# The last 64 queries of two experts in one tile of 128 rows (fused attention and mixture of experts)

## The chip, the cores and the metric

The kernel runs on one core of one Trainium2 chip. The metric is the device time of one execution in microseconds; the median of several executions counts.

## The reference

Three blocks follow each other on 4 batches of 576 tokens: a sparse attention of 8 heads, a mixing block with sines and cosines, and a mixture of four attention experts, of which each token uses two. Only the last block matters for the change:

```python
logits = x @ w_gate                       # (4, 576, 4)
topk = np.argpartition(-logits, 2, axis=-1)[..., :2]
...
for e in range(4):
    q, k, v = x @ wq[e], x @ wk[e], x @ wv[e]        # 64 wide
    scores = scale * (q @ k.transpose(0, 2, 1))
    scores = np.where(causal, -1000000000.0, scores)
    scores = scores - scores.max(-1, keepdims=True)
    a = np.exp(scores)
    a /= a.sum(-1, keepdims=True) + 1e-09
    ye = a @ v @ wo[e]
    ...
        out += mask[..., None] * w[:, :, kk:kk + 1] * ye
```

Every expert attends causally over 576 tokens, and its rows are scaled by the gate before they are added up.

## The kernel before, in words

The matrix products are done in a 32-bit format of reduced precision, and each operand is split into a high part and a low remainder, so that most products are three matmuls (hi hi, lo hi, hi lo; the helper `mm3`, lines 241 to 243). In the experts, q carries its high part in 64 partitions and its low part in the other 64; k is written twice beside that, and `klow` holds k's remainder beside 64 partitions of zeros, which are cleared once at the start of the expert stage (line 413, on POOL).

The first 382 us are the other two blocks. Then comes the expert stage, batch by batch, in `experts`. Per batch and pair of experts (m = 0, 1), `project_qk` makes q and k of both experts; then `attention` runs once per expert e. It goes over five tiles of queries, four of 128 rows and the last, t = 4, of 64. Per tile PE makes the scores (lines 514 and 515, for t = 4 in two chunks of 288 keys) and adds the causal mask by a matmul with the identity as weights (line 517). DVE takes the row maximum (519), ACT the exponential with its sum (530), DVE finishes the sum and its reciprocal (534, 535), and POOL (for t = 0 DVE) multiplies by that and by the gate (537). PE transposes the tile block by block (540) into PSUM, ACT copies it out as `pthi` (548), and DVE makes the remainder `ptlo` (549). After the five tiles PE multiplies with the values (560, 564) in two halves of 288 queries; line 569 and 570 add the two parts of v. For t = 4, all of this has 64 rows:

```python
w, t0 = TW[t], 128 * t              # TW = [128, 128, 128, 128, 64]
...
nc.tensor.matmul(s[:w, t0 - c0:t0 - c0 + w], identb[:, :w], mask_c[:, :w], ...)
...
nc.tensor.transpose(tp[:, c * w:(c + 1) * w], p[:w, 128 * c:128 * c + 128], ident[:w, :w])
```

Between the tiles stand `fill` units: the projections of the next pair and batch (`pv`, `pq`) and the output projections of the batch before (`po`), spread over 20 slots per batch. Eight output projections remain for the end. Each is copied by ACT (596) into one of four staging slots in `X[0]`, from which SP issues the store.

Names on PE: `th`, `y`, `g` belong to the mixing block, `pv`, `pq`, `po` to projections, `s` to scores, `tp` to transposes, `o` to values. The order of the instructions on each engine is set by a scheduler that plans the whole program at once when it is built. So a change in the last stage, or two copies at the start, can move rows in stages that the diff does not touch.

Of the kernel before, what the change touches and what calls it, by code (L numbers as in the profile page):

```python
# [42 lines left out]
def fused_kernel(ctx: ExitStack, tc: tile.TileContext, ql, kl, vl, qs, ks, vs, wth, wtk, wch, wqk, wvg, wo, out):  # L43
# [42 lines left out]
    select(mask_c, [[-1, 128]], 0, 1)  # L86

# [321 lines left out]
    xproj, vs, qks, moved = {}, {}, {}, []  # L409
    klow = [[cw.tile([128, S], F32R, name=f"klow_{j}_{i}") for i in range(2)] for j in range(3)]  # L410
    for j in range(3):
        for i in range(2):
            nc.gpsimd.memset(f(klow[j][i][64 - 64 * i:128 - 64 * i, :]), 0.0)

    def project_v(b):
# [7 lines left out]
        vs[b] = vc, cp.tile([128, NT, 4], F32, tag="gt", name=f"gt_{b}")  # L423
# [17 lines left out]
    def gates(b, lg):  # L441
# [20 lines left out]
        nc.vector.tensor_tensor(gt, gt, mx[:, :, 1:2].to_broadcast([128, NT, 4]), op=ALU.mult)  # L462

    def project_qk(b, m):
        q = [cp.tile([128, S], F32R, tag="q", bufs=6, name=f"q_{b}_{m}_{i}") for i in range(2)]
# [5 lines left out]
        def unit(part, n):  # L473
# [21 lines left out]
    def attention(b, e, of, fill):  # L495
        vc, gt = vs[b]
        q, k, kl = qks[b, e]
        pr = slice(64 * (e % 2), 64 * (e % 2) + 64)

        pthi = cp.tile([128, 2368], F32R, tag="pthi", name=f"pthi_{b}_{e}")  # L500
        ptlo = cp.tile([128, 2368], F32R, tag="ptlo", name=f"ptlo_{b}_{e}")
        sm = cp.tile([128, NT], F32, tag="sm", name=f"sm_{b}_{e}")
        nm = cp.tile([128, 8], F32, tag="nm", name=f"nm_{b}_{e}")
        for t in range(NT):
            w, t0 = TW[t], 128 * t
            ts = slice(t0, t0 + w)
            kn = t0 + w
            p = cp.tile([128, 640], F32, tag="p", bufs=4, name=f"p_{b}_{e}_{t}")
            chunks = [(0, kn)] if t < 4 else [(0, HALF), (HALF, S)]
            scs = []  # L510
            for ci, (c0, c1) in enumerate(chunks):
                s = ps2.tile([128, 512], F32, tag="s", bufs=3, name=f"s_{b}_{e}_{t}_{ci}")
                last = ci == len(chunks) - 1
                nc.tensor.matmul(s[:w, :c1 - c0], q[:, ts], k[:, c0:c1], start=True, stop=False)
                nc.tensor.matmul(s[:w, :c1 - c0], q[:, ts], kl[:, c0:c1], start=False, stop=not last)
                if last:
                    scored = nc.tensor.matmul(s[:w, t0 - c0:t0 - c0 + w], identb[:, :w], mask_c[:, :w],  # L517
                                              start=False, stop=True)
                nc.vector.tensor_reduce(nm[:w, t + ci:t + ci + 1], s[:w, :c1 - c0], axis=AX.X, op=ALU.max,  # L519
                                        negate=True)  # L520
                scs.append(s)
            with tc.issue_after(scored.ins):
                for unit in fill[t]:
                    unit()
            if t == 4:
                nc.vector.tensor_tensor(nm[:w, 4:5], nm[:w, 4:5], nm[:w, 5:6], op=ALU.min)
                nc.gpsimd.memset(p[:w, S:640], 0.0)
            for ci, (c0, c1) in enumerate(chunks):
                acc = sm[:w, t:t + 1] if ci == 0 else nm[:w, 6:7]
                nc.scalar.activation(p[:w, c0:c1], scs[ci][:w, :c1 - c0], AF.Exp, bias=nm[:w, t:t + 1], scale=1.0,  # L530
                                     accum_out=acc)
            if t == 4:
                nc.vector.tensor_tensor(sm[:w, 4:5], sm[:w, 4:5], nm[:w, 6:7], op=ALU.add)
            nc.vector.tensor_scalar_add(sm[:w, t:t + 1], sm[:w, t:t + 1], 1e-9)
            nc.vector.reciprocal(sm[:w, t:t + 1], sm[:w, t:t + 1])  # L535
            eng = nc.vector if t == 0 else nc.gpsimd
            eng.tensor_scalar(p[:w, :kn], p[:w, :kn], sm[:w, t:t + 1], gt[:w, t, e:e + 1], op0=ALU.mult, op1=ALU.mult)  # L537
            tp = ps2.tile([128, 512], F32, tag="t", bufs=2, name=f"tp_{b}_{e}_{t}")
            for c in range(t + 1):
                nc.tensor.transpose(tp[:, c * w:(c + 1) * w], p[:w, 128 * c:128 * c + 128], ident[:w, :w])  # L540
            src = tp[:, :(t + 1) * w].rearrange("p (n q) -> p n q", q=w)

            def dst(v):
                if t == 0:
                    return v[:, None, :w]
                return v[:, 128:128 + 448 * (t + 1)].rearrange("p (n q) -> p n q", q=448)[:, :, t0 - 128:t0 - 128 + w]
# [151 lines left out]
```

## Time and profile before

| | |
|---|---|
| median of three runs | 601.68 us (598.15 to 605.10) |
| the profiled execution | 603.8 us, its span 602.0 us |
| mean granted TensorE clock | 0.968 of full |
| busy over the span: PE, weight loads, DVE, ACT, POOL | 95%, 87%, 70%, 57%, 41% |
| expert stage | about 382 to 602 us |

The span runs from the first to the last instruction of the profiled execution; every row of the trace counts from its start. A row of the timeline tells when an instruction began, how long it is counted as busy, its engine, line and operation, and what it writes and reads. "PE" are matmuls, "PEld" their weight loads. Ends of matmuls are modelled and overlap the next, so how fast PE works is read from one start to the next. A bracket at the end tells how long the engine had been idle and which instruction ended that.

### The profile page before, as it was taken

Reading aid. Unit: us, or ns where it says so; the run is one execution under the profiler, and the core shown is the slowest. Engines: PE = TensorE matmul, PEld = TensorE weight load, DVE = VectorE, ACT = ScalarE, POOL = GpSimd, SP = SyncE. Lnnn points to the kernel's source line nnn. Section 1 sums busy time; section 2 is a strip of 40 time slices with the busy share of each in tenths; the row PEclk is TensorE's granted clock in tenths of the full one; section 3 lists DMA queues with packets and bytes.
Section 4 is the critical chain, followed back from the end, with each engine's and each line's share of the span. In section 5 each row is a group of like instructions: output and inputs, shape, how many; then the busy total and the mean of one; then the engine's idle time right before and its main releaser. Section 6 shows DMA issues by size and latency. Waiting matters only on the chain.

```text
span 602.0 us, 12582 instructions
## 1 busy us (share of the span) xinstructions
PE 571.9 (95%) x4560; PEld 525.3 (87%) x4560; DVE 422.5 (70%) x1209; ACT 340.7 (57%) x935; POOL 244.5 (41%) x336
## 2 busy tenths in 40 slices
PE   7985979899999999999999999999999999999997
PEld 5875859799999999989999999988989898989986
DVE  5689988794667646586545644289897878879881
ACT  4565796752655514646214532067577767857873
POOL 6763275441144411144300643345435624544452
PEclk9999878969999999999999999998999999999998
DMA  9723434121212111200010001100001000100112
GB/s 280 230 80 118 138 130 132 56 76 30 81 38 62 34 52 40 70 17 22 7 53 1 1 18 37 36 1 1 1 2 51 30 2 31 41 12 4 38 41 78
DMA packets 17365, 32.67 MB, mean 54 GB/s; under 512 B 2056, under 2 KB 9400, under 8 KB 17304
## 3 DMA queue, kind: packets, MB, share of 16 engines
q1 hardware_dynamic: 17304, 31.88, 17.3%
q8 instruction: 36, 0.59, 0.4%
q14 instruction: 25, 0.20, 0.1%
HBM read 27.15 MB, written 4.72 MB: 53 GB/s over the span
## 4 chain that ended last, share of the span: by engine, by line
PE 75%; DVE 12%; ACT 6%; issue 3%; DMA 2%; POOL 1%; POOLq 0%; DVEq 0%; ACTq 0%; SPq 0%
PE s L182 7%; PE y L241 6%; PE y L242 6%; PE y L243 6%; PE av L218 3%; PE tp L540 3%; PE tp L209 3%; PE g L241 3%; PE g L242 3%; PE g L243 3%; PE th L241 3%; PE th L242 2%; PE th L243 2%; PE o L564 2%; PE pq L241 2%
## 5 line engine op out<-in xcount | busy, mean ns | idle before, releaser
L241 PE MATMUL y<-wtk_hi,zhi 128*128 128x288 f32 x288 | 87.7, 305 | 0.4 <-DVE X L317 0.4
L242 PE MATMUL y<-wtk_lo,zhi 128*128 128x288 f32 x288 | 87.0, 302 | 0.0
L243 PE MATMUL y<-wtk_hi,zlo 128*128 128x288 f32 x288 | 86.2, 300 | 0.0
L302 POOL TENSOR_TENSOR zlo<-cs,zhi 128x512 fp32r<-128x512 f32 (+1 forms) x40 | 49.6, 1250 | 64.6 <-DVE zhi L299 40.2
L537 POOL TENSOR_SCALAR p<-p,sm,gt 128x256 f32<-128x256 f32 (+1 forms) x64 | 45.2, 709 | 58.8 <-DVE sm L535 44.7
L206 POOL TENSOR_TENSOR p<-p,sm 128x288 f32<-128x288 f32 (+2 forms) x48 | 33.1, 695 | 87.4 <-DVE sm L205 44.3
L530 ACT ACTIVATE p<-s,nm 128x128 f32<-128x128 f32 (+2 forms) x96 | 49.5, 517 | 14.8 <-DVE nm L519 10.0
L241 PE MATMUL th<-wth_hi,x_hi 128*128 128x256 f32 (+1 forms) x160 | 50.4, 316 | 7.2 <-DVE cs L265 6.7
L241 PEld LDWEIGHTS y<-wtk_hi,zhi 128*128 128x128 f32 x288 | 55.3, 192 | 0.7 <-DVE X L317 0.7
L242 PEld LDWEIGHTS y<-wtk_lo,zhi 128*128 128x128 f32 x288 | 55.3, 192 | 0.1
L243 PEld LDWEIGHTS y<-wtk_hi,zlo 128*128 128x128 f32 x288 | 55.2, 192 | 0.0
L237 POOL TENSOR_TENSOR x_lo<-X,x_hi 128x576 fp32r<-128x576 f32 x24 | 35.9, 1498 | 47.5 <-DVE x_hi L235 40.0
L182 PE MATMUL s<-k,qdiag 128*108 128x54 f32 (+2 forms) x320 | 54.3, 314 | 0.3 <-POOL qdiag L170 0.3
L182 PEld LDWEIGHTS s<-k,qdiag 128*108 128x108 f32 (+1 forms) x320 | 47.3, 222 | 6.5 <-issue 1.2
L519 DVE TENSOR_REDUCE nm<-s 128x1 f32<-128x128 f32 (+2 forms) x96 | 44.4, 469 | 5.4 <-PE s L517 4.1
L242 PE MATMUL th<-wth_lo,x_hi 128*128 128x256 f32 (+1 forms) x160 | 47.4, 297 | 0.0
L243 PE MATMUL th<-wth_hi,x_lo 128*128 128x256 f32 (+1 forms) x160 | 47.2, 296 | 0.0
L212 ACT COPY pt<-tp 96x384 f32<-96x384 f32 (+2 forms) x44 | 20.8, 473 | 39.6 <-PE tp L209 39.5
L241 PE MATMUL pq<-x_hi,wqk_hi 128*128 128x288 f32 x128 | 39.9, 312 | 0.7 <-DVE q L486 0.7
L549 DVE TENSOR_TENSOR ptlo<-tp,pthi 128x128 fp32r<-128x128 f32 (+4 forms) x80 | 38.1, 479 | 2.5 <-ACT pthi L548 1.9
L241 PE MATMUL g<-u_hi,wch_hi 128*128 128x288 f32 x128 | 39.3, 307 | 0.0
L241 PEld LDWEIGHTS th<-wth_hi,x_hi 128*128 128x128 f32 (+1 forms) x160 | 31.2, 195 | 8.6 <-DVE cs L265 7.6
(159 smaller groups left out, 1801.9 us busy)
## 6 DMA issues: line engine op xcount, KB each, us to landing
X<-in_wtk SPq DMA_DIRECT2D x9, 576.0 KB
out_t<-X SPq DMA_DIRECT2D x32, 144.0 KB
v<-in_vl SPq DMA_DIRECT2D x24, 144.0 KB
k<-in_kl SPq DMA_DIRECT2D x8, 304.0 KB
q<-in_ql SPq DMA_DIRECT2D x8, 288.0 KB
q<-in_qs SPq DMA_DIRECT2D x8, 288.0 KB
k<-in_ks SPq DMA_DIRECT2D x8, 288.0 KB
X<-in_wth SPq DMA_DIRECT2D x4, 512.0 KB
```

The lines of the kernel that those rows point to most:

```text
L182: nc.tensor.matmul(s[:rm, i * kw:i * kw + w], qg[:, i, :], kt[:, k0:k0 + w], start=False, stop=i == n - 1)
L206: nc.gpsimd.tensor_tensor(tiles(p), tiles(p), each(sm), op=ALU.mult)
L212: copy(pt[:kw, :n * rm], tp[:kw, :n * rm])
L237: eng.tensor_tensor(lo, x, f(hi), op=ALU.subtract)
L241: nc.tensor.matmul(ps, ahi, bhi, start=first, stop=False)
L242: nc.tensor.matmul(ps, ahi, blo, start=False, stop=False)
L243: nc.tensor.matmul(ps, alo, bhi, start=False, stop=last)
L302: nc.gpsimd.tensor_tensor(lo, zf, f(hi), op=ALU.subtract)
L519: nc.vector.tensor_reduce(nm[:w, t + ci:t + ci + 1], s[:w, :c1 - c0], axis=AX.X, op=ALU.max, negate=True)
L530: nc.scalar.activation(p[:w, c0:c1], scs[ci][:w, :c1 - c0], AF.Exp, bias=nm[:w, t:t + 1], scale=1.0, accum_out=acc)
L537: eng.tensor_scalar(p[:w, :kn], p[:w, :kn], sm[:w, t:t + 1], gt[:w, t, e:e + 1], op0=ALU.mult, op1=ALU.mult)
L549: nc.vector.tensor_tensor(dst(ptlo), src, f(dst(pthi)), op=ALU.subtract)
```

## The change

The last 64 queries of the two experts of a pair go through scores, softmax and transposes in one tile of 128 rows (`last_rows`). q gets 640 columns, 64 of them zero: for the first expert the last 64, for the second those from 512 to 575, its last 64 queries moving up behind them. A slice of columns 512 to 639 of the first q thus holds its last queries and zeros, that of the second zeros and its last queries, and matmuls of both add up in one PSUM tile. The pieces of `attention` become `rows` (four tiles), `last_rows`, and `values`. q lies in tiles that are cleared once. The transposed rows go into the `pthi` and `ptlo` of both experts. The fill slots are 18 per batch instead of 20, the staging slots three instead of four; the fourth serves as a second buffer for line 569's copy. The gate of the joint tile lies in a small tile of its own. Cut to its core:

```diff
+    mask_j = const.tile([128, 64], BF16, name="mask_j")
+    nc.vector.tensor_copy(mask_j[:64], mask_c[:64, :64])
+    nc.vector.tensor_copy(mask_j[64:], mask_c[:64, :64])
...
+    qz = [[cw.tile([128, 640], F32R, name=f"qz_{j}_{i}") for i in range(2)] for j in range(3)]
     for j in range(3):
         for i in range(2):
             nc.gpsimd.memset(f(klow[j][i][64 - 64 * i:128 - 64 * i, :]), 0.0)
+            nc.gpsimd.memset(f(qz[j][i][:, S - 64 * i:640 - 64 * i]), 0.0)
...
+        for i in range(2):
+            own = slice(64 * i, 64 * i + 64)
+            nc.vector.tensor_copy(vs[b][2][own, :], gt[:64, NT - 1, i::2])
...
-                    nc.scalar.activation(q[i][own, sl], ps, AF.Copy, scale=sc)
-                    nc.vector.scalar_tensor_tensor(q[i][other, sl], ps, sc, f(q[i][own, sl]), op0=ALU.mult,
-                                                   op1=ALU.subtract)
+                    cuts = [(0, HALF, HALF * n)] if i == 0 or n == 0 else [(0, 224, HALF), (224, HALF, S)]
+                    for a, z, to in cuts:
+                        d = slice(to, to + z - a)
+                        nc.scalar.activation(q[i][own, d], pq[own, a:z], AF.Copy, scale=sc)
+                        nc.vector.scalar_tensor_tensor(q[i][other, d], pq[own, a:z], sc, f(q[i][own, d]),
+                                                       op0=ALU.mult, op1=ALU.subtract)
...
+    def last_rows(b, m, pts, fill):
+        chunks = [(0, HALF), (HALF, S)]
+        for ci, (c0, c1) in enumerate(chunks):
+            s = ps2.tile([128, 512], F32, tag="s", bufs=3, name=f"sj_{b}_{m}_{ci}")
+            for i in range(2):
+                q, k, kl = qks[b, 2 * m + i]
+                z = q[:, 512:640]
+                nc.tensor.matmul(s[:, :HALF], z, k[:, c0:c1], start=i == 0, stop=False)
+                scored = nc.tensor.matmul(s[:, :HALF], z, kl[:, c0:c1], start=False, stop=ci == 0 and i == 1)
+            if ci == 1:
+                scored = nc.tensor.matmul(s[:, 512 - HALF:HALF], identb, mask_j, start=False, stop=True)
+            nc.vector.tensor_reduce(st[:, ci:ci + 1], s[:, :HALF], axis=AX.X, op=ALU.max, negate=True)
+            scs.append(s)
+        p = softmax_tile(b, f"{b}_{m}_j", scs, chunks, st, st[:, 2:3], vs[b][2][:, m:m + 1], scored, fill)
+        for c0, c1 in ((0, 4), (4, 5)):
+            tp = ps2.tile([128, 512], F32, tag="t", bufs=2, name=f"tpj_{b}_{m}_{c0}")
+            for c in range(c0, c1):
+                nc.tensor.transpose(tp[:, 128 * (c - c0):128 * (c - c0) + 128], p[:, 128 * c:128 * c + 128], ident)
+            for i in range(2):
+                src = tp[:, :128 * (c1 - c0)].rearrange("p (n q) -> p n q", q=128)[:, :, 64 * i:64 * i + 64]
+                hi, lo = (v[:, 128:].rearrange("p (n q) -> p n q", q=448)[:, c0:c1, 384:] for v in pts[i])
+                nc.scalar.copy(hi, src)
+                nc.vector.tensor_tensor(lo, src, f(hi), op=ALU.subtract)
...
-            for e in (2 * m, 2 * m + 1):
-                attention(b, e, of, fill[NT * e:NT * e + NT])
+            rows(b, e0, pts[0], fill[9 * m:9 * m + 4])
+            pts.append(new_pt(b, e1))
+            last_rows(b, m, pts, fill[9 * m + 4])
+            values(b, e0, pts[0], of)
+            rows(b, e1, pts[1], fill[9 * m + 5:9 * m + 9])
+            values(b, e1, pts[1], of)
...
-        i = 4 * n + m
-        ot = X[0][:, 2 + i % 2, HALF * (i // 2 % 2):HALF * (i // 2 % 2) + HALF]
+        i = (4 * n + m) % 3
+        ot = X[0][:, 2 + i // 2, HALF * (i % 2):HALF * (i % 2) + HALF]
```

Three places show what this does to the order of the instructions. On PE, the last batch, second pair, before the change: the last tile of expert 2 is transposed, and the second chunk of scores of expert 3's last tile follows with its mask (`s_3_4_1`).

```order
L560 MATMUL o_2_0_7803<-ptlo_2_7694,vc_6929 64x32
L564 MATMUL o_2_0_7803<-pthi_2_7693,vc_6929 128x32
L540 MATMUL tp_2_4_7795<-ident,p_2_4_7777 128x64 x5
L514 MATMUL s_3_4_1_7916<-k_1_1_7356,q_1_1_7354 64x288
L515 MATMUL s_3_4_1_7916<-klow_1_4732,q_1_1_7354 64x288
L517 LDWEIGHTS identb
L517 MATMUL s_3_4_1_7916<-mask_c,identb 64x64
L540 MATMUL tp_3_0_7850<-ident,p_3_0_7831 128x128
```

The same pair with the change: the transposes of the joint tile (`tpj`), in two PSUM tiles, stand among the values of expert 2.

```order
L608 MATMUL o_2_0_7726<-pthi_2_7594,vc_6862 128x288
L583 MATMUL tpj_1_0_7711<-ident,p_1_j 128x128 x4
L604 MATMUL o_2_0_7726<-ptlo_2_7595,vc_6862 64x288
L608 MATMUL o_2_0_7726<-pthi_2_7594,vc_6862 128x160
L604 MATMUL o_2_0_7726<-ptlo_2_7595,vc_6862 64x160
L604 MATMUL o_2_0_7726<-ptlo_2_7595,vc_6862 64x32
L608 MATMUL o_2_0_7726<-pthi_2_7594,vc_6862 128x32
L583 MATMUL tpj_1_4_7720<-ident,p_1_j 128x128
L608 MATMUL o_2_1_7736<-pthi_2_7594,vc_6862 128x288
```

Ten transposes of 64 columns per pair have become five of 128, the joint scores stand well ahead of them, and no tile of 64 rows is left. On POOL, the start of the expert stage with the change: the clearing of `klow` and `qz`, then of the logits `lg`.

```order
L109 TENSOR_TENSOR wvg_lo<-wvg_st_4329,wvg_hi 128x260
L418 MEMSET klow_0_4738 64x576
L419 MEMSET qz_0_4732 128x64
L418 MEMSET klow_1_4739 64x576
L419 MEMSET qz_1_4733 128x64
L418 MEMSET klow_0_4740 64x576
L419 MEMSET qz_0_4734 128x64
L418 MEMSET klow_1_4741 64x576
L419 MEMSET qz_1_4735 128x64
L418 MEMSET klow_0_4742 64x576
L419 MEMSET qz_0_4736 128x64
L418 MEMSET klow_1_4743 64x576
```

The six memsets of `qz` are new, one behind each of `klow`; the last `qz` and then `lg` follow. On DVE in the opening, before the change: the first angles (`cs_0_0`) behind the decoding of the weights `wtk` (`X` from lines 132 to 135).

```order
L132 TENSOR_SCALAR X_100<-X_100 128x576
L133 TENSOR_SCALAR X_100<-X_100 128x576
L134 SCALAR_TENSOR_TENSOR X_100<-X_101,X_100 128x576
L264 TENSOR_SCALAR cs_0_0_655<-th_0_0_642 128x256
L264 TENSOR_SCALAR cs_0_1_672<-th_0_1_659 128x256
L194 TENSOR_REDUCE mx_0_0_1003<-s_0_0_998 128x3
L135 SCALAR_TENSOR_TENSOR X_100<-X_101,X_100 128x576
```

With the change:

```order
L136 TENSOR_SCALAR X_103<-X_103 128x576
L137 TENSOR_SCALAR X_103<-X_103 128x576
L138 SCALAR_TENSOR_TENSOR X_103<-X_104,X_103 128x576
L139 SCALAR_TENSOR_TENSOR X_103<-X_104,X_103 128x576
L198 TENSOR_REDUCE mx_0_0_1006<-s_0_0_1001 128x3
L268 TENSOR_SCALAR cs_0_0_658<-th_0_0_645 128x256
L136 TENSOR_SCALAR X_103<-X_103 128x576
```

The fourth decoding step and a row maximum have moved ahead of the first angles; many rows of this stage have changed places like these.

## Rows read from the trace of the kernel before

**Rows 1.** Busy time by stretch: PE, PEld, DVE, ACT, POOL, clock, DMA, GB/s

```profile
399.00:420.00 21.00, 19.77 (x137) 17.47 (x136) 19.52 (x62) 16.94 (x52) 13.29 (x19) 0.92 0.01 2
420.00:580.00 160.00, 158.53 (x1229) 144.51 (x1228) 134.68 (x484) 115.05 (x349) 71.93 (x124) 1.00 0.07 23
```

**Rows 2.** Groups by line and shape, 400 to 602 us: busy, mean ns, idle before

```profile
L519 DVE TENSOR_REDUCE nm<-s 64x1 f32<-64x288 f32 x32 | 14.2, 444 | 3.2 <-PE s L517 2.4 <-PE s L515 0.3
...
L514 PEld LDWEIGHTS s<-k,q 128*128 128x128 f32 x62 | 11.7, 192 | 1.0 <-POOL k L491 0.6
...
L540 PE MATMUL tp<-ident,p 64*128 64x64 f32 x80 | 8.8, 234 | 0.0
...
L514 PEld LDWEIGHTS s<-k,q 128*64 128x64 f32 x32 | 4.4, 139 | 1.1 <-ACT p L530 0.9
...
L517 PE MATMUL s<-mask_c,identb 128*64 128x64 bf16 x16 | 3.5, 217 | 0.0
```

**Rows 3.** Timeline of PE around a last tile's transposes and mask: start, busy

```profile
572.95 0.29 PE L242 MATMUL po<-olo,wo_hi 128*128 128x288 f32 x1
573.09 0.29 PE L243 MATMUL po<-ohi,wo_lo 128*128 128x288 f32 x1
573.31 0.52 PE L540 MATMUL tp<-ident,p 64*128 64x64 f32 x5
573.76 0.35 PE L560 MATMUL o<-ptlo,vc 128*64 128x288 f32 x1
...
574.77 0.29 PE L515 MATMUL s<-klow,q 128*64 128x288 f32 x1
575.00 0.22 PE L517 MATMUL s<-mask_c,identb 128*64 128x64 bf16 x1
575.14 0.33 PE L514 MATMUL s<-k,q 128*128 128x128 f32 x1
```

**Rows 4.** Timeline of PE around transposes and masks of 128-row tiles

```profile
508.48 0.61 PE L540 MATMUL tp<-ident,p 128*128 128x128 f32 x4
508.84 0.42 PE L514 MATMUL s<-k,q 128*128 128x384 f32 x1
509.10 0.33 PE L515 MATMUL s<-klow,q 128*128 128x384 f32 x1
509.27 0.23 PE L517 MATMUL s<-mask_c,identb 128*128 128x128 bf16 x1
509.31 0.48 PE L514 MATMUL s<-k,q 128*128 128x512 f32 x1
509.62 0.40 PE L515 MATMUL s<-klow,q 128*128 128x512 f32 x1
509.86 0.23 PE L517 MATMUL s<-mask_c,identb 128*128 128x128 bf16 x1
```

**Rows 5.** Timeline of POOL, DVE and PE at the start of the expert stage

```profile
382.77 3.64 POOL L413 MEMSET klow<- 64x576 f32 x6 [13.57 <-PE g L243]
...
386.36 0.11 POOL L420 MEMSET lg<- 128x20 f32 x1
...
386.50 0.16 DVE L435 COPY lg<-pv 128x4 f32<-128x4 f32 x1 [0.62 <-POOL lg L420]
...
386.81 0.36 PE L241 MATMUL pv<-wvg_hi,x_hi 128*128 128x260 f32 x1 [0.48 <-DVE lg L435]
```

**Rows 6.** Timeline of PE and ACT in the last stretch

```profile
586.84 0.41 PE L564 MATMUL o<-pthi,vc 128*128 128x288 f32 x1 [0.72 <-ACT pthi L548]
...
589.66 0.37 PE L564 MATMUL o<-pthi,vc 128*128 128x288 f32 x1 [1.11 <-DVE X L570]
...
597.96 0.40 ACT L596 COPY X<-po 128x288 f32<-128x288 f32 x1 [0.39 <-PE po L243]
...
598.78 0.40 ACT L596 COPY X<-po 128x288 f32<-128x288 f32 x1 [0.41 <-PE po L243]
```

**Rows 7.** Timeline of PE in the opening

```profile
60.04 0.58 PE L241 MATMUL th<-wth_hi,x_hi 128*128 128x256 f32 x1 [5.62 <-DVE cs L265]
```

More of the change, by code (lines that the diff above doesn't have):

```diff
@@ L462, in gates @@
         nc.vector.tensor_tensor(gt, gt, mx[:, :, 1:2].to_broadcast([128, NT, 4]), op=ALU.mult)
+        for i in range(2):
+            own = slice(64 * i, 64 * i + 64)
+            nc.vector.tensor_copy(vs[b][2][own, :], gt[:64, NT - 1, i::2])
     def project_qk(b, m):
-        q = [cp.tile([128, S], F32R, tag="q", bufs=6, name=f"q_{b}_{m}_{i}") for i in range(2)]
+        q = qz[(2 * b + m) % 3]
         k = [cp.tile([128, S], F32R, tag="k", bufs=5, name=f"k_{b}_{m}_{i}") for i in range(2)]
@@ L493, in project_qk @@
         return unit
-    def attention(b, e, of, fill):
-        vc, gt = vs[b]
-        q, k, kl = qks[b, e]
[L498 to L537, printed above, removed]
@@ new lines, in softmax_tile @@
+    def softmax_tile(b, name, scs, chunks, nm, sm, gate, after, fill):
+        p = cp.tile([128, 640], F32, tag="p", bufs=4, name=f"p_{name}")
+        kn = chunks[-1][1]
+        with tc.issue_after(after.ins):
+            for unit in fill:
+                unit()
+        if len(chunks) > 1:
+            nc.vector.tensor_tensor(nm[:, 0:1], nm[:, 0:1], nm[:, 1:2], op=ALU.min)
+            nc.gpsimd.memset(p[:, S:640], 0.0)
+        for ci, (c0, c1) in enumerate(chunks):
+            acc = sm if ci == 0 else nm[:, 1:2]
+            nc.scalar.activation(p[:, c0:c1], scs[ci][:, :c1 - c0], AF.Exp, bias=nm[:, 0:1], scale=1.0, accum_out=acc)
+        if len(chunks) > 1:
+            nc.vector.tensor_tensor(sm, sm, nm[:, 1:2], op=ALU.add)
+        nc.vector.tensor_scalar_add(sm, sm, 1e-9)
+        nc.vector.reciprocal(sm, sm)
+        eng = nc.vector if kn == 128 else nc.gpsimd
+        eng.tensor_scalar(p[:, :kn], p[:, :kn], sm, gate, op0=ALU.mult, op1=ALU.mult)
+        return p
@@ new lines, in new_pt, with rows @@
+    def new_pt(b, e):
+        return tuple(cp.tile([128, 2368], F32R, tag=tag, name=f"{tag}_{b}_{e}") for tag in ("pthi", "ptlo"))
+    def rows(b, e, pt, fill):
+        vc, gt, _ = vs[b]
+        q, k, kl = qks[b, e]
+        pthi, ptlo = pt
+        st = cp.tile([128, 12], F32, tag="st", name=f"st_{b}_{e}")
+        for t in range(4):
+            t0 = 128 * t
+            ts = slice(t0, t0 + 128)
+            kn = t0 + 128
+            s = ps2.tile([128, 512], F32, tag="s", bufs=3, name=f"s_{b}_{e}_{t}")
+            nc.tensor.matmul(s[:, :kn], q[:, ts], k[:, :kn], start=True, stop=False)
+            nc.tensor.matmul(s[:, :kn], q[:, ts], kl[:, :kn], start=False, stop=False)
+            scored = nc.tensor.matmul(s[:, t0:kn], identb, mask_c, start=False, stop=True)
+            nm = st[:, 3 * t:3 * t + 2]
+            nc.vector.tensor_reduce(nm[:, 0:1], s[:, :kn], axis=AX.X, op=ALU.max, negate=True)
+            p = softmax_tile(b, f"{b}_{e}_{t}", [s], [(0, kn)], nm, st[:, 3 * t + 2:3 * t + 3], gt[:, t, e:e + 1], scored,
+                             fill[t])
@@ L548, in attention @@
             nc.scalar.copy(dst(pthi), src)
             nc.vector.tensor_tensor(dst(ptlo), src, f(dst(pthi)), op=ALU.subtract)
+    def last_rows(b, m, pts, fill):
+        st = cp.tile([128, 3], F32, tag="stj", name=f"stj_{b}_{m}")
+        chunks = [(0, HALF), (HALF, S)]
+        scs = []
+        for ci, (c0, c1) in enumerate(chunks):
+            s = ps2.tile([128, 512], F32, tag="s", bufs=3, name=f"sj_{b}_{m}_{ci}")
[18 more added lines that the diff above has]
+                nc.vector.tensor_tensor(lo, src, f(hi), op=ALU.subtract)
@@ L550, in attention, with values @@
+    def values(b, e, pt, of):
+        vc = vs[b][0]
+        pthi, ptlo = pt
+        pr = slice(64 * (e % 2), 64 * (e % 2) + 64)
         for n in range(2):
@@ L567, in attention @@
                     low()
-            tmp = cp.tile([64, HALF], F32, tag="tmp", name=f"tmp_{b}_{e}_{n}")
+            if n == 0:
+                tmp = cp.tile([64, HALF], F32, tag="tmp", bufs=1, name=f"tmp_{b}_{e}")
+            else:
+                tmp = X[0][:64, 3, HALF:]
             nc.scalar.copy(tmp, o[64:128, :HALF])
@@ L616, in spread @@
     def spread(units, first, last):
-        out = [[] for _ in range(NE * NT)]
+        out = [[] for _ in range(18)]
         for i, u in enumerate(units):
```

17 lines of the change are left out of this document (10 added, 7 removed).

## Prediction

> **What bounds the kernel now.** I read four views, in this order. First the busy time by stretch: from 420 to 580 us, which is the steady part of the expert stage, PE is busy 158.53 of 160.00 us at the full granted clock (the factor 1.00, which is the 2.4 GHz level), while DVE has 134.68, ACT 115.05 and POOL 71.93 [rows 1]. So PE sets the pace there, and a microsecond taken off another engine is worth nothing unless PE happens to wait for it. A busy PE is not yet a PE at its peak, though. The rows of one matmul overlap those of the next, so the second view is PE's own timeline, and the number to read in it is the distance from one start to the next. A matmul of 288 moving columns follows the last at 0.13 to 0.14 us (572.95 to 573.09) [rows 3]; that is what streaming costs. Anything above it is a cost of changing from one kind of work to another. Third, the timeline where the expert stage begins, with the wait that the memsets on POOL cause, and fourth the waits at the end and in the opening [rows 5 to 7].
>
> **The change, part by part.** There are 16 experts (4 batches times 4), hence 16 last tiles of 64 queries; they become 8 joint tiles of 128 rows.
>
> *Masks on PE.* Each last tile ends with a mask matmul, 64 weight columns and 64 moving columns, 16 in all [rows 2]. Around it, the scores matmul at 574.77 is followed only 0.23 us later (0.13 would be streaming, so 0.10 is extra), and the mask itself holds the next matmul off for 0.14 (575.00 to 575.14) [rows 3]: 0.24 us per mask. With 128 weight columns, as in the other four tiles, the same step is cheaper: the mask at 509.27 holds the next start for 0.04, and the scores matmul after it, 512 columns, takes 0.31 where its twin takes 0.24, so 0.07 to 0.08 is paid late: 0.12 in all [rows 4]. The joint mask has 128 weight columns and 64 moving ones, so I price it at 0.12, not less. 16 x 0.24 - 8 x 0.12 = 3.84 - 0.96 = 2.9 us off PE. If the joint mask behaved like the old ones it would still be 8 x 0.24 = 1.9.
>
> *Transposes on PE.* Five transposes of 64 columns per expert, 80 in all [rows 2]. From the last ordinary matmul before such a run (573.09) to the first after it (573.76) there are 0.67 us, of which 0.13 is that matmul: 0.54 per run [rows 3]. Four transposes of 128 columns take 0.36 (508.48 to 508.84) and 0.09 more in the matmul behind them (0.26 where its twin of the same 384 columns takes 0.17): 0.45, or 0.11 each [rows 4]. A joint tile has five of these, 0.56. 16 x 0.54 - 8 x 0.56 = 8.64 - 4.5 = 4.1 us off PE. Splitting the five over two PSUM tiles, so that other matmuls stand between, could cost one more 0.09 per pair, 0.7 us in all; I leave it at the upper end of the range.
>
> *Scores on PE.* Eight matmuls of 288 columns per pair before and after: the zero columns in q save no streaming and cost none. What grows is the weight load, 64 columns before and 128 now, 139 against 192 ns for each of 64 loads [rows 2], 53 ns x 64 = 3.4 us if nothing covered it. In the output projection, 288-column matmuls with 128-column weights still start every 0.14 us [rows 3], so the load lies under the matmul ahead of it. I take 0 and keep 3.4 as an end. The Trainium skill, in "TensorE: Matmul & The Clock Gate", section "LDWEIGHTS (loading the stationary operand)", lets the load grow with the number of columns, and "Perfetto Trace Analysis", section "Identifying the Most-Contended Engine", would have TensorE judged by the busy share of its loads and not of its matmuls. The trace agrees on the growth, and that share is 144.51 of 160.00 here; read as the bound it speaks against the change, by the 3.4 us already named, while the unchanged start-to-start distance speaks for cover.
>
> *DVE, ACT, POOL.* A pair loses two of four row maxima (444 ns each) [rows 2] and two of four exponentials, one of two sets of small sums, and one of two gate multiplications. In exchange the copies out of PSUM are cut finer: four and four instead of two and two. All of it lies beside a PE that is busy 99% of the time, so I count 0. The cover would be gone only where PE waits, at the beginning and the end.
>
> *q, gates, masks.* One q piece per pair is written in two parts, one more instruction each on ACT and DVE, and two small gate copies per batch are added; both lie in the same shadow, 0. The two copies that build the joint mask stand on DVE ahead of the mask that PE's first matmul needs; at 0.16 us, the price of the small copy in [rows 5], they cost 0 to 0.3, and I take 0.1, because PE then waits for POOL anyway.
>
> *The zero columns.* Six memsets of 64 columns are woven between the six of 576 columns on POOL, ahead of the one that clears the logits. This queue is on the path: the six take 3.64 us, the clearing follows at 386.36, the copy on DVE at 386.50 waited 0.62 for it, and PE waited 0.48 for that copy [rows 5]. A memset costs 0.11 for 20 columns and 0.61 for 576 [rows 5]; in proportion 64 columns come to 0.15, an estimate, and 6 x 0.15 = 0.9 us, all of it added to PE's 0.48. The ends are 0.7 and 3.6.
>
> *Stores.* Three staging slots instead of four. In the last stretch the copies come every 0.82 us (597.96, 598.78) [rows 6], so a slot is wanted again after 2.46. The last copy ends at 599.18 and the span at 602.00, so a store with all that follows it takes at most 2.8. If the whole of that held a slot, a copy would wait 2.8 + 0.4 - 2.5 = 0.7, twice in the tail: 0 to 1.5 us. The 2.8 include the end of the program, so I take 0.
>
> *The end.* The last expert now finishes with its 512-column tile; no short tile follows. Before, PE waits 0.72 us for ACT and 1.11 for DVE there [rows 6]. One stage of softmax fewer on DVE and ACT should take something from the first of these; I take 0.5 off, with ends of +1 and -1.8.
>
> The sum: -2.9 - 4.1 + 0.1 + 0.9 - 0.5 = -6.5 us. The profiled execution took 603.8 us (span 602.0), so 597.3 by its measure. It stands 2.1 above the median of the runs shown, 601.68, and against that median I predict 595.2.
>
> **Rivals.**
>
> *The weight loads are not covered.* Then 3.4 of the 6.5 go: -3.1, 598.6 us. For it speaks the load share of 90% [rows 1]; against it the start distances [rows 3].
>
> *The waits go too.* From 399 to 420 us DVE is busy 19.52 of 21.00, PE idles 1.23 and its mean granted clock is 0.92, so part of it ran at the 1.2 GHz level, worth 0.08 x 21 = 1.7 us [rows 1]. If the joint tile relieves DVE enough that PE does not wait there, 2.9 more come back, and at the end the rest of the 1.83 of waits: -6.5 - 2.9 - 1.3 = -10.7, 591.0 us. Against it: the extra memsets and the finer copies fall into just that stretch.
>
> *The opening gets worse.* The orders above show rows moved on DVE before the first angles, long before the expert stage, and all engines are reordered there. PE's longest wait of the whole run is there, 5.62 us at 60.04, for DVE [rows 7]. Two more weight-decoding rows now stand ahead of the first angle operation. If later waits of that sort follow, so that the wait is paid twice more, 11.2 us are added: -6.5 + 11.2 = +4.7, 606.4 us. From 6.5 us of new waits this rival decides the sign. Against it: the two rows alone are some 1.2 us, and rows that move later elsewhere can as well shorten a wait.
>
> *A new wait for the joint tile.* It is between the two experts, and the values of the first now need it. But PE has other work queued between its scores and its transposes in every pair, so I fold this into the width of the range.
>
> **How the numbers follow.** Chances: forecast 0.48 (its own range 593 to 598), uncovered loads 0.14, waits that go too 0.23, a worse opening 0.15. A measurement of this kernel can tell about 1%, 6 us, from no change. The forecast lies just beyond that bound and gives 0.27 to faster and 0.21 to same; the loads give all to same; the third gives all to faster; the opening is split between same and slower. Together 0.50, 0.42 and 0.08. The range goes from 589.5, a little past the third, to 602.5, leaving out most of the opening.
>
> **What would show it.** Right: PE's transposes in this stage become all 128 columns wide, 200 of them, with no run costing 0.54; the 64-column weight loads of the scores are gone and 288-column scores still start every 0.13 to 0.14; the six new memsets are near 0.15 each and PE's wait for the logits' copy is near 1.4 us; from 420 to the end PE's stretch is shorter by 6 to 7 us at the same busy share. Wrong: scores that start every 0.19, PE idle in the middle of the stage ahead of the joint transposes, or a first memset of the stage that begins at another time than 382.77 [rows 5], which would put the difference into the stages before.

## The result, and the profile after

The changed kernel takes 606.36 us (median of 20 runs, 603.83 to 607.37), the kernel before 600.94 (20 runs, 598.15 to 605.10): a ratio of 1.0081, 95% interval 1.0063 to 1.0100. It is slower by 0.8% where 595.2 and faster had been forecast. The profiled execution took 606.1 us (span 604.3).

Busy time by stretch, changed kernel, in the columns of [rows 1] (a name, the stretch's length, PE, PEld, DVE, ACT, POOL, clock, DMA, GB/s):

```profile
384.00:420.00 36.00, 32.53 (x245) 30.07 (x246) 25.61 (x97) 20.88 (x61) 18.97 (x39) 1.00 0.05 16
420.00:580.00 160.00, 151.86 (x1173) 141.75 (x1172) 131.52 (x467) 110.31 (x340) 65.86 (x111) 0.99 0.07 23
580.00:604.30 24.30, 17.95 (x122) 15.93 (x121) 9.58 (x30) 11.04 (x32) 6.97 (x11) 0.90 0.16 56
```

PE did get less to do: 151.86 us busy from 420 to 580 where it was 158.53 [rows 1]. But the work that it lost became idle time: 8.1 us of it in 160, where there had been 1.5. PE's waits over the stage, changed kernel (who, waiting for what: us in all, times, longest):

```profile
PE o L608 <- DVE X L617: 2.6, 3, 1.0
PE tpj L583 <- DVE st L523: 1.4, 2, 1.2
PE tp L552 <- POOL p L526: 1.3, 1, 1.3
PE pv L245 <- DVE lg L442: 1.1, 1, 1.1
...
PE s L543 <- POOL k L505: 0.9, 1, 0.9
PE o L608 <- ACT pthi L560: 0.9, 1, 0.9
...
```

The same view of the kernel before:

```profile
PE o L564 <- DVE X L570: 1.1, 1, 1.1
PE o L564 <- ACT pthi L548: 0.7, 1, 0.7
PE s L514 <- ACT p L530: 0.7, 1, 0.7
...
```

The first list has 16 rows and 14.9 us in all, the second 11 rows and 6.4. No single wait took the place of the old ones; they are many, each near 1 us, for many different things.

To put a number on both sides I took every matmul's distance to the next start in the timeline, from the first value projection to the last output projection, and subtracted what its columns need to stream (0.13 us for 288, and 0.11 for a transpose of 128). It is counted in matmuls' starts, so no modelled end enters. Excess up to 0.25 us I call an *edge* (a change from one kind of work to another), more than that a *gap* (a wait); steps of 288 columns that start every 0.24 us ran at half the full clock and are counted as neither.

| kernel | stage, us | edges | gaps |
|---|---|---|---|
| before | 215.2 | 29.7 | 9.5 |
| changed | 216.5 | 20.5 | 19.8 |

9.2 us of edges went, 10.3 us of gaps came (with the line between them at 0.5 instead of 0.25 us it is 8.0 and 9.2). The stage became 1.3 us longer in these two profiles, whose spans lie 2.3 us apart. The medians lie 5.4 us apart; where the rest arises, only further runs can tell.

### The profile page after: what moved, and what is told of

Its sections match the earlier page's. It is cut to its first block, busy times and chain, and to the rows that moved or that the text cites. A ratio compares the mean times of both kernels' runs of the same rounds, so it can differ in the third digit from the quotient of the medians.

```text
span 604.3 us, 12430 instructions
## 1 busy us (share of the span) xinstructions
PE 560.6 (93%) x4512; PEld 517.1 (86%) x4512; DVE 416.2 (69%) x1195; ACT 335.7 (56%) x927; POOL 239.1 (40%) x326
## 5 line engine op out<-in xcount | busy, mean ns | idle before, releaser
L210 POOL TENSOR_TENSOR p<-p,sm 128x288 f32<-128x288 f32 (+2 forms) x48 | 35.2, 740 | 73.6 <-DVE sm L209 43.8
L186 PEld LDWEIGHTS s<-k,qdiag 128*108 128x108 f32 (+1 forms) x320 | 45.6, 215 | 10.7 <-issue 5.8
L186 PE MATMUL s<-k,qdiag 128*108 128x54 f32 (+2 forms) x320 | 53.0, 308 | 0.0
L526 POOL TENSOR_SCALAR p<-p,st,gt 128x256 f32<-128x256 f32 (+2 forms) x48 | 32.8, 686 | 40.5 <-DVE st L524 15.9
L520 ACT ACTIVATE p<-s,st 128x128 f32<-128x128 f32 (+1 forms) x64 | 34.1, 533 | 12.8 <-DVE st L547 9.7
L222 PE MATMUL av<-pt,v 54*64 54x54 f32 (+2 forms) x640 | 34.0, 252 | 5.0 <-ACT X L230 1.9
L222 PEld LDWEIGHTS av<-pt,v 54*64 54x64 f32 (+2 forms) x640 | 27.1, 159 | 13.4 <-issue 4.9
L608 PE MATMUL o<-pthi,vc 128*128 128x288 f32 (+4 forms) x128 | 34.5, 292 | 3.7 <-DVE X L617 2.6
```

What stands on the lines that cost most here:

```text
L186: nc.tensor.matmul(s[:rm, i * kw:i * kw + w], qg[:, i, :], kt[:, k0:k0 + w], start=False, stop=i == n - 1)
L210: nc.gpsimd.tensor_tensor(tiles(p), tiles(p), each(sm), op=ALU.mult)
L222: nc.tensor.matmul(av[64 * h:64 * h + 64, i * rw:i * rw + wd[i]], vg[:w, i, h, :], pt[:w, i, h, :wd[i]], start=True, stop=True)
L520: nc.scalar.activation(p[:, c0:c1], scs[ci][:, :c1 - c0], AF.Exp, bias=nm[:, 0:1], scale=1.0, accum_out=acc)
L526: eng.tensor_scalar(p[:, :kn], p[:, :kn], sm, gate, op0=ALU.mult, op1=ALU.mult)
L608: nc.tensor.matmul(o[:, a - q0:HALF], vc[:, c, e].rearrange("p a d -> p (a d)"), pthi[:, cols], start=c == 0, stop=last)
```

## The experiments

Theory "waits": PE's saving is real and comes back as waits in the stage. Rivals: the opening ate it; the memsets on POOL did; the edges merely moved ("price").

**The opening, from both sides.** In the first run the copies wait on DVE for the first logits copy of the expert stage; in the second they are put into the kernel before, and nothing else is.

```
 # e1_mask_late
     mask_j = const.tile([128, 64], BF16, name="mask_j")
-    nc.vector.tensor_copy(mask_j[:64], mask_c[:64, :64])
-    nc.vector.tensor_copy(mask_j[64:], mask_c[:64, :64])
...
-            nc.vector.tensor_copy(lg[:w, t, :], pv[:w, 256:260])
+            copied = nc.vector.tensor_copy(lg[:w, t, :], pv[:w, 256:260])
+            if b == 0 and t == 0:
+                with tc.issue_after(copied.ins):
+                    nc.vector.tensor_copy(mask_j[:64], mask_c[:64, :64])
+                    nc.vector.tensor_copy(mask_j[64:], mask_c[:64, :64])
 # e8_before_copies, in the kernel before
     select(mask_c, [[-1, 128]], 0, 1)
+    mask_j = const.tile([128, 64], BF16, name="mask_j")
+    nc.vector.tensor_copy(mask_j[:64], mask_c[:64, :64])
+    nc.vector.tensor_copy(mask_j[64:], mask_c[:64, :64])
```

> The two copies that build the joint mask wait on DVE until the first logits copy of the expert stage, so that all engines run the opening in the order of before. Theory 'waits' (the 6.5 us that PE saves in the expert stage are real, but come back there as waits of PE for the softmax chain; the opening costs only the 1.0 us by which the stage starts later, 384.16 against 383.20): about 1.0 us off the changed kernel, ratio to it 0.998, first pv matmul near 383.2, stage as long as in the changed kernel (220 us). Rival 'opening' (the opening is what eats the gain): 6 us or more off, below 600.

> The kernel before with nothing added but the two copies of the joint mask in the opening (the tile is built and not used). The engines then run the opening in the changed kernel's order and the expert stage in that of before. Theory 'order of the opening' (the copies shift what DVE, ACT and PE do between 10 and 110 us, and that costs 3.5 to 4 us by itself): 604.5 to 605.5, ratio 1.006. Rival (the opening costs only together with the expert stage's new tiles, or the 1.0 us of the profiled runs is all there is): at most 602.5, ratio under 1.002.

With late copies 602.3 us, ratio to before 1.0023 (1.0001 to 1.0045): 4.1 us off the changed kernel (3.5 by the ratios), four times the 1.0 expected. The kernel before with the copies 604.3, ratio 1.0056 (1.0033 to 1.0079): 3.1 us, with an untouched expert stage, a little under the 604.5 to 605.5 expected. Ahead of the expert stage the rows of PE, DVE, ACT and POOL stand in the first run in the order of the kernel before, in the second in that of the changed kernel, without an exception. Both agree on 3 to 4 us, and both expectations that took the 1.0 us between two profiles for the cost were wrong. Stretches of the opening, first late copies, then before with the copies:

```profile
60.00:110.00 50.00, 45.47 (x345) 40.02 (x346) 41.82 (x97) 40.01 (x111) 22.33 (x21) 0.84 0.38 120
```

```profile
60.00:110.00 50.00, 39.54 (x317) 34.61 (x318) 41.73 (x101) 40.26 (x107) 23.94 (x21) 0.86 0.40 120
```

PE is busy 5.9 us less there at about the same clock, and DVE and ACT as much as ever. Its longest waits, before with the copies:

```profile
PE s L182 <- DVE mask_l L68: 4.4, 1, 4.4
PE s L182 <- ACT p L200: 3.2, 1, 3.2
PE xn L283 <- DVE cs L293: 3.0, 1, 3.0
PE th L245 <- DVE cs L269: 2.9, 2, 2.3
PE th L245 <- ACT X L230: 2.6, 1, 2.6
```

The 5.62 us of [rows 7] fell to 2.3, and waits for ACT stand in its place: another order of all engines, not a longer wait of the same kind. The first row is PE's first matmul: it starts at 4.36 us where it started at 3.89, so 0.5 us are the plain delay by the two copies, 0.16 and 0.17 us on DVE. The rest of the 3 to 4 us comes with the other order that is fixed after them, since nothing else differs.

**The memsets.** They stand on POOL behind the clearing of the logits and of the last value tile; the rest of the order is that of the changed kernel, row for row.

```
-            nc.gpsimd.memset(f(qz[j][i][:, S - 64 * i:640 - 64 * i]), 0.0)
...
+        cleared = nc.gpsimd.memset(f(vc[64:128, NT - 1]), 0.0)
+        if b == 0:
+            with tc.issue_after(cleared.ins):
+                for j in range(3):
+                    for i in range(2):
+                        nc.gpsimd.memset(f(qz[j][i][:, S - 64 * i:640 - 64 * i]), 0.0)
```

> The six memsets of zero columns stand on POOL behind the clearing of the logits and of the last value tile, all else in the order of the changed kernel. PE's wait for the first logits copy (1.1 us there, 0.5 before) falls back to 0.5. Theory 'waits': 0.6 us off, ratio 0.999, too little to tell from none. Rival 'memsets' (POOL's queue carries them on): 3 us or more off.

606.06 us, ratio to before 1.0085 (1.0065 to 1.0105): no difference from the changed kernel. PE's wait for the logits' copy is 0.5 again, as expected. The memsets are not the cause.

**Is the saving real?** Both kernels with transposes that read the identity, so that PE's transposes never wait for a softmax.

```
 # e3_joint_const: late copies, late memsets, and (the joint tile's transposes likewise)
-                nc.tensor.transpose(tp[:, 128 * c:128 * c + 128], p[:, 128 * c:128 * c + 128], ident)
+                nc.tensor.transpose(tp[:, 128 * c:128 * c + 128], ident, ident)
 # e4_before_const
-                nc.tensor.transpose(tp[:, c * w:(c + 1) * w], p[:w, 128 * c:128 * c + 128], ident[:w, :w])
+                nc.tensor.transpose(tp[:, c * w:(c + 1) * w], ident[:w, :], ident[:w, :w])
```

> The changed kernel with the mask copies and the memsets moved as in the two runs above, and with every softmax transpose of the expert stage reading the identity instead of the probabilities: PE no longer waits for maxima, exponentials and gates, DVE, ACT and POOL do the same work as before. The output is left wrong by this. Read against the next run, which does the same to the kernel before. Theory 'waits': PE's saving shows, 4 to 7 us shorter than the next run. Rival 'price' (the new order's edges on PE cost what the masks and transposes saved): within 2 us of it.

> The kernel before, with every softmax transpose of the expert stage reading the identity instead of the probabilities (the output is left wrong by this). Theory 'waits': it gains less from this than the changed kernel does, since PE waits only about 10 us in its stage, against 18: 3 to 8 us off the kernel before. Rival 'price': both gain the same.

593.95 against 594.30 us: within 2 us, so by its totals the rival "price" came true and mine did not. (Against 602.3 and 601.49 without the identity, the changed form gained 8.4 us and the kernel before 7.2.) The timeline tells them apart better. Edges are 19.6 against 27.5, so 7.9 are saved, nearly as in the full kernels; gaps are 13.1 against 6.5. So the saving on edges is real. The waits came back although no transpose waited for a softmax. The first waits of the changed form (late copies, identity):

```profile
PE po L243 <- ACT X L655: 2.8, 3, 2.0
PE s L549 <- POOL k L511: 2.1, 3, 1.3
PE pv L245 <- DVE x_lo L239: 1.5, 2, 1.0
PE s L549 <- ACT p_j L526: 1.1, 1, 1.1
```

Two kinds are to be seen. PE needs an operand that was made shortly before (k, x_lo), or it begins a tile whose PSUM buffer another engine has not read out: an output projection reads nothing of the staging copy X that it waits for, and scores read nothing of the exponential p_j.

**The joint tile's own chain.** The runs of this part and the next have the late copies.

```
 # e6_values_late
-            values(b, e0, pts[0], of)
             rows(b, e1, pts[1], fill[9 * m + 5:9 * m + 9])
+            values(b, e0, pts[0], of)
 # e7_joint_first
...
-            rows(b, e0, pts[0], fill[9 * m:9 * m + 4])
-            pts.append(new_pt(b, e1))
-            last_rows(b, m, pts, fill[9 * m + 4])
...
+            last_rows(b, m, pts, fill[9 * m])
+            rows(b, e0, pts[0], fill[9 * m + 1:9 * m + 5])
```

> The changed kernel with the opening of before, and with the first expert's values behind the second expert's four tiles, so that the joint tile's softmax, transposes and eight copies have a whole expert's scores beside them. Theory 'joint tile's chain' (the first expert's values now wait for the joint tile): 3 to 6 us under 602.3. Rival 'thin cover': no gain, or up to 2 us more, since both experts' values then stand together at the end of a pair with nothing beside them.

> The changed kernel with the opening of before, and with the joint tile ahead of the first expert's four tiles instead of behind them. Theory 'joint tile's chain': 3 to 6 us under 602.3, and the last pair ends as in the changed kernel. Rival 'late fills': the joint tile needs all of both experts' q and k at once, so the wait for them grows, and it is 1 to 5 us slower than 602.3.

604.22 us (ratio 1.0049, 1.0023 to 1.0074) and 611.23 (1.0157, 1.0120 to 1.0193): no gain, as the rival "thin cover" had it, and a loss of 8.9 us, more than either side expected. Freeing the first expert's values from the joint tile gains nothing. Both edits also move other work, so they do not show that this chain costs nothing.

**The fills.** The projections are woven between the tiles by slot. The change made 18 slots of 20 and kept the ranges in proportion.

```
 # e5_fill_early: both; e11_next_only: the second; e13_pair_only: the first
-            spread(units_qk(b, 1), 0, 8 if b else 4), spread(done, 0, 9 if b + 1 < B else 18),
-            spread(units_v(b + 1) + units_qk(b + 1, 0) if b + 1 < B else [], 9 if b else 5, 18))]
+            spread(units_qk(b, 1), 0, 7 if b else 4), spread(done, 0, 9 if b + 1 < B else 18),
+            spread(units_v(b + 1) + units_qk(b + 1, 0) if b + 1 < B else [], 8 if b else 5, 17))]
```

> The changed kernel with the opening of before (mask copies late), and with the projections of the next experts one slot earlier (the next pair's over slots 0 to 7 instead of 0 to 8, the next batch's over 8 to 17 instead of 9 to 18). Theory 'late fills' (PE's new waits come from q, k and value tiles that are projected too short before their use): 3 to 6 us under the 602.3 of the run with late mask copies. Rival 'thin cover' (PE has too little other work beside the softmax chain wherever it stands): within 1.5 us of it.

> The run with early fills with one of its two edits alone: the next batch's projections over 8 to 17, the next pair's over 0 to 8 as in the changed kernel. If the last k of a batch is what came late (the changed kernel issues it in slot 17, the last; before, in slot 18 of 0 to 19), this alone gives most of the 4.8 us: 597.5 to 599. If the second pair's tiles are the late ones, it gives little: 601 to 602.5.

> The changed kernel with the opening of before and the other of the two edits alone: the next pair's projections over slots 0 to 7, the next batch's over 9 to 18 as in the changed kernel. The run with the next batch's alone gained nothing (603.5 against 602.3). Theory 'the second pair's k is late' (its last unit stands in slot 6; with the joint tile in slot 4 two slots are left before the pair begins, three before the change): 597.5 to 599. Rival 'both are needed' (each moves a bare place): 601 to 603.

Both together 597.47 us, ratio 0.9933 (0.9907 to 0.9960): 4.8 off the run with late copies, and faster than before. The next batch's alone 603.53 (1.0058, 1.0034 to 1.0081): no gain, outside both ranges expected. The pair's alone 601.24 (1.0009, 0.9983 to 1.0034): 1.1 off. So neither of the single theories holds; by the times both are needed. Gaps went from 20.5 (late copies) to 18.8, 17.7 and, with both, 15.6, nearly the sum of the two. One place shows how such waits arise. PE, POOL and ACT of the changed kernel where the second pair's last k is made:

```profile
519.43 0.30 PE L247 MATMUL pq<-x_hi,wqk_lo 128*128 128x288 f32 x1
...
522.14 0.40 PE L608 MATMUL o<-pthi,vc 128*128 128x288 f32 x1 [0.85 <-ACT pthi L560]
523.45 0.44 PE L543 MATMUL s<-k,qz 128*128 128x384 f32 x1 [0.90 <-POOL k L505]
```

```profile
520.42 1.42 POOL L241 TENSOR_TENSOR x_lo<-X,x_hi 128x576 fp32r<-128x576 f32 x1 [3.74 <-ACT x_hi L237]
521.83 1.05 POOL L526 TENSOR_SCALAR p<-p,st,gt 128x256 f32<-128x256 f32 x1
522.97 0.43 POOL L505 TENSOR_SCALAR k<-k 64x288 fp32r<-64x288 f32 x1
```

```profile
519.62 1.23 ACT L237 CAST x_hi<-X 128x576 fp32r<-128x576 f32 x2
520.76 0.39 ACT L503 CAST k<-pq 64x288 fp32r<-64x288 f32 x1
521.04 0.67 ACT L237 CAST x_hi<-X 128x576 fp32r<-128x576 f32 x1
521.62 0.95 ACT L560 CAST pthi<-tp 128x384 fp32r<-128x384 f32 x2
...
522.89 0.39 ACT L503 CAST k<-pq 64x288 fp32r<-64x288 f32 x1
```

PE ends the projection near 519.7. The copies of k stand on ACT among the splits of the next batch's x (0.67 each) and on POOL behind another (1.42) and a gate multiplication; `pthi` stands on ACT behind the same splits. PE waits for both, twice within 1.5 us. In this profile the price is more than the 1.75 of the two: from 518 to 529 the granted clock falls to 0.84, so part of the stretch ran at the 1.2 GHz level, while the kernel before held 1.00 there. Clocks of that place, in the order changed, before, next batch's alone, pair's alone:

```profile
518.00:529.00 11.00, 9.24 (x58) 8.27 (x57) 8.54 (x22) 7.88 (x21) 6.54 (x9) 0.84 0.08 29
```

```profile
518.00:529.00 11.00, 10.74 (x84) 9.57 (x83) 10.04 (x27) 8.96 (x25) 7.37 (x11) 1.00 0.12 41
```

```profile
514.00:527.00 13.00, 11.24 (x74) 10.04 (x74) 9.94 (x26) 8.64 (x25) 7.22 (x10) 0.87 0.11 37
```

```profile
511.00:522.00 11.00, 10.08 (x77) 9.39 (x77) 10.24 (x29) 10.08 (x30) 6.50 (x8) 1.00 0.17 56
```

With the pair's units one slot ahead the first of the two waits is gone and the clock stays at its upper level; measured against the same amount of streaming, 2.7 us return at this place. But the fall of the clock does not follow from the two waits alone. The run with late memsets has all of PE's rows in the changed kernel's order and both waits at this place, and its clock held:

```profile
523.02 0.40 PE L612 MATMUL o<-pthi,vc 128*128 128x288 f32 x1 [0.85 <-ACT pthi L564]
524.33 0.45 PE L547 MATMUL s<-k,qz 128*128 128x384 f32 x1 [0.91 <-POOL k L509]
```

```profile
519.00:530.00 11.00, 9.24 (x71) 8.29 (x70) 9.08 (x24) 8.09 (x22) 7.42 (x10) 1.00 0.12 42
```

Row against row it passes this place 1.5 us faster than the changed kernel, and its stage takes 214.5 us. So 1.5 us are the clock's share, and about 1.2 of the 2.7 are left for the wait. Of five profiles with both waits here (changed, e1, e2, e6, e11) the clock fell in four; in six with one or neither (e5, e10, e13 to e16) it held. The pair's run lost 1.9 us again at its very end, at the 1.2 GHz level:

```profile
584.00:588.00 4.00, 2.68 (x12) 2.24 (x12) 1.37 (x3) 0.98 (x2) 1.23 (x2) 0.50 0.03 6
588.00:592.00 4.00, 3.99 (x18) 3.64 (x17) 0.45 (x1) 1.20 (x3) 1.23 (x2) 0.50 0.12 42
```

There too the waits do not settle it: with both ranges moved PE has the same two waits of 0.85 us just before, and the clock held 1.00 up to 584.

**Do the terms add?** The changed kernel, opening included, with both ranges of e5:

> The changed kernel as it was, opening included, with only the two ranges of the fills moved (0 to 7, 8 to 17). If the terms add, 606.4 less 4.8: 601 to 602.5, no longer to be told from the kernel before. Rival 'the terms do not add' (the opening's loss is partly one of the stage): 603.5 to 605.

602.52 us, ratio 1.0015 (0.9992 to 1.0039): 3.8 off, just above the 601 to 602.5 expected. The two causes are nearly independent, and with the second one mended the changed kernel can no longer be told from the one before.

**What is the joint tile worth with all placed well?** The ranges for the changed form (late copies) and for the kernel before:

```
 # e10_fill_earlier: pair 0 to 6, next batch 7 to 16
 # e14_best, e16_best_again: late memsets, pair 0 to 6, next batch 8 to 17
 # e9_before_early: pair 0 to 8, next batch 9 to 19 (before: 0 to 9, 10 to 20)
 # e17_before_earlier: pair 0 to 7, next batch 9 to 19
```

> The run with early fills (597.5), with the fills one slot earlier still: the next pair's over 0 to 6, the next batch's over 7 to 16. Theory 'late fills': what was late is now early enough, and little more is to be had: 595 to 598. Rival 'thin cover' (each advance only moves the bare places): the last two slots of a batch now have no fill, and it is 2 to 5 us slower than 597.5.

> The kernel before with the same advance of its fills: the projections of the next pair over slots 0 to 8 instead of 0 to 9, those of the next batch over 9 to 19 instead of 10 to 20. Theory 'late fills belong to the change' (with 18 slots for 20 the last k comes one tile nearer to its use, and only there it is late; before, PE has gaps of 9.5 us in the whole stage): within 1.5 us of the kernel before. Rival 'the advance is good anyway' (it has nothing to do with the joint tile): 3 to 5 us under the kernel before, and then the joint tile gains nothing even with it.

> All that helped together: mask copies late, memsets late, the next pair's projections over slots 0 to 6, the next batch's over 8 to 17. Theory 'late fills', terms that add: 597.5 less 0.3 for the memsets, 596.5 to 598, ratio to before 0.992 to 0.995. Rival 'thin cover': no better than the run with early fills, 598 to 600.

> The best form of the change (opening of before, late memsets, fills over 0 to 6 and 8 to 17), on one chip with the next run. Theory 'edges': the joint tile saves 9 us of matmul edges and still pays some 6 us of waits more, so against a kernel before with equally early fills it stays 1 to 4 us ahead. Rival 'nothing left': within 1 us of the next run, and the joint tile is worth nothing even when all is placed well.

> The kernel before with the next pair's projections over slots 0 to 7 instead of 0 to 9 and the next batch's over 9 to 19 instead of 10 to 20. With the advance by one slot it took 598.4; two slots for the pair should give little more: 597 to 599.5. Theory 'edges': 1 to 4 us above the run ahead of this one. Rival 'nothing left': within 1 us of it.

597.75 us (ratio 0.9949, 0.9923 to 0.9975), 598.41 (0.9967, 0.9939 to 0.9995), 597.49 (0.9956, 0.9930 to 0.9982), and, on one chip, 596.67 (0.9935, 0.9912 to 0.9959) against 598.24 (0.9958, 0.9935 to 0.9982). So early fills are good for the kernel before too, by 2 to 3 us, between the two expectations of e9, and what stays for the joint tile is 1.6 us with intervals that overlap: a gain that is not shown. By the profiles:

| kernel | stage, us | edges | gaps |
|---|---|---|---|
| best form (e16) | 209.8 | 19.6 | 15.2 |
| before, early fills (e17) | 210.3 | 26.8 | 8.2 |

7.2 us of edges saved, 7.0 of gaps added, even here. The longest waits that stay in the best form:

```profile
PE o L614 <- DVE X L623: 1.9, 2, 1.0
PE pq L243 <- DVE qz L506: 1.6, 3, 0.7
PE po L243 <- ACT X L655: 1.1, 2, 0.9
PE pv L243 <- DVE klow L510: 0.9, 1, 0.9
```

None of these four reads what it waits for; each begins a PSUM tile that DVE or ACT still reads out. That points to read-out as what paces the stage once PE is quicker. No run changed the read-out alone, so this stays argued.

## Why the prediction was wrong

*Masks and transposes, -7.0:* right, even low. Edges fell by 9.2. The joint mask and what follows it, and the five transposes, changed kernel:

```profile
504.53 0.29 PE L573 MATMUL sj<-k,qz 128*128 128x288 f32 x1
504.67 0.30 PE L574 MATMUL sj<-klow,qz 128*128 128x288 f32 x1
504.80 0.20 PE L576 MATMUL sj<-mask_j,identb 128*128 128x64 bf16 x1
504.84 0.38 PE L245 MATMUL po<-ohi,wo_hi 128*128 128x288 f32 x1
505.06 0.29 PE L246 MATMUL po<-olo,wo_hi 128*128 128x288 f32 x1
```

```profile
487.30 0.71 PE L583 MATMUL tpj<-ident,p_j 128*128 128x128 f32 x5
487.76 0.34 PE L604 MATMUL o<-ptlo,vc 128*64 128x160 f32 x2
487.95 0.26 PE L608 MATMUL o<-pthi,vc 128*128 128x32 f32 x1
```

0.04 for the mask and 0.09 in the matmul behind it (0.22 for 0.13): 0.13, where 0.12 was said. The five transposes take 0.46, and the 192 columns behind them 0.19 where streaming takes 0.09: 0.56, as was said. All 200 transposes of the stage are 128 columns wide now, as the prediction's sign for being right has it.

*Scores covered, 0:* right; the joint scores follow each other at 0.13 to 0.14 us (504.53, 504.67, 504.80), so the larger weight loads lie under the matmuls. The Trainium skill ("Perfetto Trace Analysis", section "Identifying the Most-Contended Engine") takes the loads' busy share, beside the share of peak arithmetic, as the measure of how near TensorE is to its limit. Here that share fell from 144.51 to 141.75 of 160 while the stage grew, so it told nothing of the loss.

*DVE, ACT and POOL, 0, "all of it lies beside a PE that is busy 99% of the time":* this step failed in the stage. The 99% were taken as proof that PE sets the pace by itself. A busy PE contains its edges, and while PE pays them the other engines go on. With 9.2 us of edges gone, 10.3 of gaps took their place; that the edges had been the others' time to catch up is my reading of this. The text folded a new wait into the width because "PE has other work queued between its scores and its transposes in every pair", and looked at the joint tile alone; e6 finds no gain in freeing the values from it, and e5, e11 and e13 find that the fills, re-spread over 18 slots, are nearly half of it (20.5 to 15.6, where the kernel before has 9.5). What paces the rest stays open; read-out of PSUM is argued above, not shown. The range could have held this step by itself: with the opening of before the changed form takes 602.3, just inside its end of 602.5.

*Opening, 0 to 0.3 for two copies:* this step failed too, and by 3 to 4 us; even the plain delay of PE's first matmul was 0.5. The rival "the opening gets worse" had the place and the sign, but not the mechanism: the 5.62 us wait did not come twice more, it shrank to 2.3 at most. That its 606.4 met the measured 606.36 is luck, since it kept the whole -6.5 of the stage and added 11.2. It also took the rows that moved ahead of the first angles for two decoding rows; the orders show one decoding row and one row maximum. The prediction's own sign for it, a first memset that begins elsewhere than at 382.77, was seen, at 383.73:

```profile
383.73 0.57 POOL L418 MEMSET klow<- 64x576 f32 x1 [13.54 <-PE g L247]
384.36 0.16 POOL L419 MEMSET qz<- 128x64 f32 x1
...
387.94 0.11 POOL L426 MEMSET lg<- 128x20 f32 x1
```

*Memsets, +0.9:* the new ones take 0.14 to 0.16, as estimated; PE's wait for the logits' copy is 1.1, where 1.4 was said; from the first memset to the logits' clearing there are 4.21 us where there were 3.59 [rows 5], so +0.6, and e2 finds no loss that the runs can tell.

*Stores, 0:* right; ACT's copies at the end still come every 0.8 us and wait for PE alone. *End, -0.5:* wrong in sign. From 570 us on PE waits 3.7 us where it waited 2.3, and from the last q and k projection to the last output projection it takes 30.5 us instead of 30.0. Two waits for DVE's sum into X, 0.85 and 1.03, stand there now, where there was one of 1.11; the one of 0.72 for `pthi` [rows 6] went, and one of 0.85 for `ptlo` came.

*Rival "the waits go too":* one part came true, the clock. From 384 to 420 us the changed kernel held 1.00, where [rows 1] has 0.92 from 399 to 420, its 1.7 us; the kernel before with early fills alone (e9) held 1.00 there too.

The sum by measured terms, against 600.94: the opening +3.1 (e8), the stage +0.8 (e1, which has the opening of before, against its own 601.49) to +1.3 (the two profiles), 604.8 to 605.3 of 606.36. The rest lies within the interval of e8 alone, 2.0 to 4.7 us. A single profile's stage is no surer than the 1.5 us of clock that came and went between the changed kernel and e2.

## What to carry to other kernels

An engine that is busy 99% of the time need not be the only bound: before counting a saving on it, count what the engines that feed it and empty its buffers can do in the shorter time, above all where what PE needs stands behind other work in their order. When the number of slots or the order of a fill changes, look at each producer's distance to its consumer again; here one slot was worth 5 us to the change and 2 to the kernel before. And a small edit far ahead of the stage that is meant, if it moves an order that is fixed afterwards, is to be tried by itself.

## What was not expected of the hardware

The opening is not repeated exactly. With the same order of instructions, the profiled executions of the late-copies run and of the best form reach the expert stage at 380.7 and 385.7 us. From 110 to 160 us PE is equally busy in both, at another mean clock; first late copies, then the best form:

```profile
110.00:160.00 50.00, 47.88 (x408) 43.62 (x407) 39.15 (x85) 24.21 (x51) 18.49 (x15) 0.93 0.25 70
```

```profile
110.00:160.00 50.00, 47.88 (x379) 43.65 (x377) 36.89 (x80) 23.57 (x52) 18.09 (x15) 0.86 0.21 61
```

Over all profiles of this case that stretch shows 0.86, 0.90, 0.93 or 0.97. 0.07 of 50 us are 3.5 us of full-speed work. The kernel before was profiled at 0.90 and the changed one at 0.97 there, enough to explain that their starts of the stage lie only 1.0 us apart while the runs say 3 to 4. Over all profiles the opening's loss shows again: with the opening of before the stage starts at 382.4 us on average (14 profiles, 379.9 to 385.7), with the changed one at 385.0 (4 profiles, 384.2 to 385.6).
